# A sparse attention and maxout kernel: v in four overlapping chunks, six copies from GpSimd, and loads in order of use

## The chip, the cores and the metric

The kernel runs on one core of a Trainium2 chip. The metric is the time of one execution on the device in microseconds. A run's profile covers one execution; its span is one to two microseconds shorter than the time. TensorE does the matmuls and transposes, VectorE and ScalarE work on tiles, GpSimd ("POOL" in the profile) is a general engine, and SyncE ("SP") issues most DMA transfers. Each engine has its instructions in a fixed order, which a scheduler chooses when the program is built.

## The reference

Four batches of 8 heads, 768 positions and head size 64. Each query sees the keys within 15 positions of it, and 24 block summaries (the maximum of the keys and the mean of the values of each 32 positions). The heads' outputs are joined to rows of 512, which go through a maxout layer.

```python
k_sum = k.reshape(B, H, nb, 32, D).max(axis=3)
v_sum = v.reshape(B, H, nb, 32, D).mean(axis=3)
scores_l = where(abs(i - j) < 16, scale * q @ k.T, -1e9)
scores_s = scale * q @ k_sum.T + log(32)
a = softmax(concatenate([scores_l, scores_s]))
x = a @ concatenate([v, v_sum])           # joined over heads: [3072, 512]
out = maximum(x @ w1, x @ w2) @ w_out     # d_ff = 1024
```

## The kernel before

For each batch, `k` and `q` are loaded, cast and transposed pair by pair of heads. A tile of 64 queries needs 96 keys around it (two interleaved halves, `j`, of 48 rows of position pairs) and the 24 summaries: 120 rows, which `kext` (keys) and `vext` (values) hold for each of the 12 query tiles. `sc` are the scores, `prob` their exponentials times a 0/1 mask, `av` the product with `vext`, `x` the normalised result and `xt` its transpose, eight of them for a batch. The maxout uses `max(a, b) = a + relu(b - a)`: `wd = w2 - w1` gives `h` and `g = relu(h)`; `w1o = w1 @ w_out` is made once on the chip from `w1b` (w1 in bf16), `w1t` (its transpose) and `wo` (w_out in bf16). The maxout of one batch alternates with the attention of the next.

The values reach `vext` in this way: VectorE casts v into `vb`, with rows of position pairs in three chunks of 128. A window of 48 rows can straddle two chunks, so 16 copies within SBUF are needed for a batch, all issued by SyncE:

```python
def prep_v(b):
    vbt, vx = vb[b % 2], vext[b % 2]
    for hp in range(NP):
        nc.vector.tensor_copy(out=vbt[..., 2 * hp:2 * hp + 2, 0:D]..., in_=by_slot(loads["vf", b, hp]))
    for j in range(2):
        r = j * 48
        nc.sync.dma_start(out=vx[r:r + 48, 0], in_=vbt[0:48, 0, j])
        nc.sync.dma_start(out=vx[r:r + 48, 1:NT:4], in_=vbt[24:72, :, j])
        # ... six more copies
    ps = psum.tile([128, H, D], F32, tag="tr", bufs=2, name="vs_ps")
    # ... six matmuls with amean: block means; VectorE copies them to vx[96:NK, 0]
    nc.sync.dma_start(out=vx[96:NK, 1:NT]..., in_=vx[96:NK, 0:1]...to_broadcast(...))   # "the broadcast"
```

`kext` gets its 24 block maxima by a small GpSimd copy for each pair of heads ("the block-maximum copy"). The eight PSUM banks are `tr` 2, `sc` 2, `av` 1, `h` 2, `o` 1. The order in the program is: load batch 0, `prep_v(0)`, load the weights, attention of batch 0, cast the weights, make `w1o`, and then for each batch: load the next batch, `prep_v` of it, maxout with the next attention as its filling.

The softmax here doesn't subtract the row's maximum and nothing guards it: scores larger than these inputs give would overflow.

## Time and profile before

| | before |
|---|---|
| time, median of 3 runs | 225.22 us (224.93 to 225.33) |
| span of the profile | 224.2 us |
| TensorE busy | 174.6 us (78%) |
| first `x` started / last `xt` of batch 0 written | 37.8 / 60.2 us |
| outputs' last tile written to SBUF | 221.4 us |

In the page's second part each digit is the busy share, in tenths, of one of 40 slices of the span (5.6 us each here); PEclk is the granted TensorE clock in tenths. These are three rows of it, of the kernel before:

```profile
PE   0003832665788999896989999999999999999973
...
PEclk9999999997699999999999999999999999999999
DMA  6998438999997335999634599634431101202112
```

TensorE is full from about 80 us on. What can be won lies before that: TensorE does nothing for three slices and little up to 62 us. The DMA row shows a hole in slices 5 and 6.

The table of stretches of the same kernel: the stretch in us, its length, then the busy time and the number of instructions of PE, PEld, DVE, ACT and POOL; then the TensorE clock, the mean busy share of the DMA engines and GB/s:

```profile
0.00:20.00 20.00, 0.00 (x0) 0.10 (x1) 7.94 (x12) 1.28 (x1) 15.35 (x45) 1.00 1.01 270
20.00:40.00 20.00, 10.76 (x81) 7.56 (x81) 11.22 (x23) 8.12 (x11) 1.16 (x2) 1.00 0.55 162
40.00:62.00 22.00, 14.84 (x171) 10.95 (x172) 20.44 (x48) 11.06 (x16) 0.86 (x2) 0.84 1.04 328
62.00:80.00 18.00, 16.43 (x117) 8.88 (x116) 12.30 (x25) 6.09 (x12) 1.05 (x2) 1.00 0.68 179
80.00:115.00 35.00, 32.08 (x301) 19.19 (x304) 21.11 (x56) 17.94 (x32) 0.86 (x2) 1.00 0.78 209
```

From 20 to 40 us the DMA engines were busy for 0.55 of the time. From 40 to 62 us VectorE is busy 20.4 of 22 us and looks like the limit there. After 62 us the DMA engines have time to spare (0.68, 0.78). The timeline of SyncE (start, duration, instruction) says why there is a hole:

```profile
20.36 0.63 SPq L188 DMA_DIRECT2D vext_115<-vb_113  x1
...
31.47 0.60 SPq L195 DMA_DIRECT2D vext_115<-vb_113  x1
32.18 0.82 SPq L202 DMA_DIRECT2D vext_115<-vext_115  x1
33.05 0.53 SPq L154 DMA_DIRECT2D w2f<-in_moe_w_dram  x1
```

The sixteen copies take SyncE from 20.36 to 32.1 us. The broadcast of the means and the rest of the weights stand behind them. In the waits of TensorE (total, times, longest) the first full group of `av` waits for that broadcast, and the first `x` follows it on VectorE's timeline:

```profile
PE av L277 <- DMA vext_115<-vext_115: 4.1, 1, 4.1
```

```profile
37.79 0.56 DVE L284 TENSOR_TENSOR x<-av,inv 128x384 bf16<-128x384 f32 x1
```

### The profile page before, as it was taken

Reading aid. Unit: us, or ns where it says so; the run is one execution under the profiler, and the core shown is the slowest. Engines: PE = TensorE matmul, PEld = TensorE weight load, DVE = VectorE, ACT = ScalarE, POOL = GpSimd, SP = SyncE. Lnnn points to the kernel's source line nnn. Section 1 sums busy time; section 2 is a strip of 40 time slices with the busy share of each in tenths; the row PEclk is TensorE's granted clock in tenths of the full one; section 3 lists DMA queues with packets and bytes.
Section 4 is the critical chain, followed back from the end, with each engine's and each line's share of the span. In section 5 each row is a group of like instructions: output and inputs, shape, how many; then the busy total and the mean of one; then the engine's idle time right before and its main releaser. Section 6 shows DMA issues by size and latency. Waiting matters only on the chain.

```text
span 224.2 us, 3831 instructions
## 1 busy us (share of the span) xinstructions
PE 174.6 (78%) x1475; PEld 103.8 (46%) x1496; DVE 118.0 (53%) x268; ACT 102.7 (46%) x173; POOL 23.9 (11%) x61
## 2 busy tenths in 40 slices
PE   0003832665788999896989999999999999999973
PEld 0001622543553655664555466655546664544531
DVE  5432852899972950896857069844727853000000
ACT  2000651575120573585179248824935972442521
POOL 8990110000000010000011001000000000000000
PEclk9999999997699999999999999999999999999999
DMA  6998438999997335999634599634431101202112
GB/s 187 289 290 273 106 100 251 375 365 283 288 281 183 90 90 135 288 292 282 184 117 102 158 259 306 163 116 152 103 87 50 51 0 47 96 0 95 47 47 94
DMA packets 49858, 37.68 MB, mean 168 GB/s; under 512 B 2192, under 2 KB 44720, under 8 KB 49840
## 3 DMA queue, kind: packets, MB, share of 16 engines
q1 hardware_dynamic: 49840, 37.45, 58.5%
q8 instruction: 11, 0.18, 0.3%
q14 instruction: 7, 0.06, 0.1%
HBM read 25.17 MB, written 6.29 MB: 140 GB/s over the span
## 4 chain that ended last, share of the span: by engine, by line
PE 49%; DMA 15%; DVE 13%; ACT 11%; SPq 7%; issue 3%; POOL 1%; ACTq 0%; POOLq 0%
PE o_ps L343 16%; DMA vf<-in_v_dram 13%; PE h_ps L330 11%; PE o_ps L339 8%; PE av L277 4%; PE sc L253 2%; ACT g L332 2%; PE x_ps L294 2%; DMA vext_115<-vext_115 2%; DVE wd L161 2%; SPq L127 2%; ACT qbd_107 L242 2%; PE vs_ps L199 2%; ACT qbd_108 L242 2%; PE w1o_ps L174 2%
## 5 line engine op out<-in xcount | busy, mean ns | idle before, releaser
L330 PE MATMUL h_ps<-xt,wd 128*128 128x384 bf16 x256 | 54.2, 331 | 2.5 <-DVE xt L296 1.1
L343 PE MATMUL o_ps<-wo,g 128*128 128x512 bf16 x186 | 46.5, 379 | 0.3
L332 ACT ACTIVATE g<-h_ps 128x384 bf16<-128x384 f32 x64 | 30.1, 491 | 15.7 <-PE h_ps L330 15.2
L347 ACT COPY osb<-o_ps 128x512 f32<-128x512 f32 x24 | 14.1, 586 | 49.2 <-PE o_ps L343 49.1
L330 PEld LDWEIGHTS <-wd 128*128 128x128 bf16 x256 | 23.7, 98 | 16.8 <-issue 3.0
L343 PEld LDWEIGHTS <-g 128*128 128x128 bf16 x192 | 17.9, 98 | 18.2
L339 PE MATMUL o_ps<-w1o,xt 128*128 128x512 bf16 x83 | 24.1, 378 | 2.1 <-ACT osb L347 1.4
L199 PE MATMUL vs_ps<-vb_113,amean 128*128 128x512 bf16 x12 | 4.2, 502 | 20.4 <-DVE vb_113 L182 20.4
L282 DVE RECIPROCAL inv<-av 128x6 f32<-128x6 f32 x32 | 6.1, 190 | 25.0 <-PE av L277 24.9
L284 DVE TENSOR_TENSOR x<-av,inv 128x384 bf16<-128x384 f32 x32 | 17.6, 550 | 0.3
L234 DVE TENSOR_REDUCE ks<-k_ps 128x24 bf16<-128x768 bf16 x16 | 15.1, 945 | 0.0
L162 ACT CAST wo<-wof 128x1024 bf16<-128x1024 f32 x4 | 4.2, 1043 | 23.8 <-DMA wof<-in_moe_w_out_dram 23.8
L339 PEld LDWEIGHTS <-xt 128*128 128x128 bf16 x96 | 9.1, 97 | 10.4 <-issue 4.0
L199 PEld LDWEIGHTS <-amean 128*128 128x128 bf16 x24 | 2.5, 107 | 24.3 <-issue 13.8
L296 DVE COPY xt<-x_ps 128x384 bf16<-128x384 bf16 x32 | 11.3, 352 | 2.8 <-PE x_ps L294 2.2
L294 PE MATMUL x_ps<-identity,x 128*128 128x128 bf16 x96 | 11.2, 230 | 1.4 <-ACT qbd_108 L242 0.6
L242 ACT COPY qbd_107<-q_ps 64x768 bf16<-64x768 bf16 x10 | 7.9, 792 | 9.3 <-PE q_ps L219 9.2
L255 ACT ACTIVATE prob_109<-sc,bias 120x512 bf16<-120x512 f32 x12 | 8.3, 689 | 7.8 <-PE av L277 6.7
L242 ACT COPY qbd_106<-q_ps 64x768 bf16<-64x768 bf16 x12 | 9.5, 793 | 4.0 <-PE q_ps L219 3.9
L213 DVE CAST qb<-qf 128x768 bf16<-128x768 f32 x16 | 10.3, 647 | 1.1 <-DMA qf<-in_q_dram 1.1
L182 DVE CAST vb_113<-vf 128x768 bf16<-128x768 f32 x8 | 5.1, 638 | 10.4 <-DMA vf<-in_v_dram 10.3
L219 PE MATMUL k_ps<-identity,kb 128*128 128x128 bf16 x96 | 9.8, 236 | 1.0 <-DVE ks L234 0.9
(94 smaller groups left out, 251.0 us busy)
## 6 DMA issues: line engine op xcount, KB each, us to landing
kf<-in_k_dram SPq DMA_DIRECT2D x16, 384.0 KB
qf<-in_q_dram SPq DMA_DIRECT2D x16, 384.0 KB
vf<-in_v_dram SPq DMA_DIRECT2D x16, 384.0 KB
out_dram<-osb SPq DMA_DIRECT2D x24, 256.0 KB
w1f<-in_moe_w_dram SPq DMA_DIRECT2D x4, 512.0 KB
wof<-in_moe_w_out_dram SPq DMA_DIRECT2D x4, 512.0 KB
w2f<-in_moe_w_dram SPq DMA_DIRECT2D x4, 512.0 KB
vext_115<-vb_113 SPq DMA_DIRECT2D x8, 148.5 KB
```

The lines of the kernel that those rows point to most:

```text
L199: nc.tensor.matmul(out=ps[:], lhsT=amean[:, c, :], rhs=vbt[:, c, j, :, 0:D], start=(c == 0 and j == 0), stop=(c == 2 and j == 1))
L213: nc.vector.tensor_copy(out=qb[:], in_=by_slot(loads["qf", b, hp]))
L234: nc.vector.tensor_reduce(out=ks[:], in_=kps.rearrange("p j (n g) -> p n j g", g=16), axis=AX.XY, op=ALU.max)
L242: nc.scalar.copy(out=qx[r, :, a * 64:a * 64 + 64].rearrange("p t (g j) -> p t g j", j=2), in_=qps[r].rearrange("p j (t g) -> p t g j", g=32))
L284: nc.vector.tensor_tensor(out=x[:], in0=av[:, :, :, 0:D], in1=inv[:].to_broadcast([128, 3, 2, D]), op=ALU.mult)
L294: nc.tensor.transpose(out=ps[:, u, :], in_=xs[half][:, u].rearrange("p a d -> p (a d)"), identity=identity[:])
L296: nc.vector.tensor_copy(out=xts[b, half][:, hp, :], in_=ps[:].rearrange("p u n -> p (u n)"))
L330: nc.tensor.matmul(out=h[:], lhsT=wd[:, c, f * 128:f * 128 + 128], rhs=xt[:, c, :], start=(c == 0), stop=(c == KC - 1))
L332: nc.scalar.activation(out=g[:, f, :], in_=h[:], func=ACT.Relu)
L339: nc.tensor.matmul(out=ps[:], lhsT=xt[:, c, sl], rhs=w1o[:, c, :], start=(c == 0), stop=False)
L343: nc.tensor.matmul(out=ps[:], lhsT=g[:, f, sl], rhs=wo[:, f, :], start=False, stop=(f == FC - 1))
L347: nc.scalar.copy(out=o[:, u, :], in_=ps[:])
```

## The change

The intent: cut v into four chunks that overlap by 16 rows (112 rows each, at steps of 96), so that every window lies in one chunk, at one of three offsets in it; six copies then do what sixteen did, and one mask serves all tiles. GpSimd does the casts and issues the copies, so SyncE is free for loads; v is loaded whole, early, and the weights in halves in order of use. `vs_ps`, `w1o`, `h` and `o` share two banks (`mm`), and `av` gets two.

```diff
+    AVB, MMB, WFB = 2, 2, 8
+    NU, VP = 4, 112
+    vf = [const.tile([VP, H, 128], F32, name=f"vf{u}") for u in range(NU)]
     # ... one mask [128, 64]; edge rows of kext and vb set to zero; memsets moved to VectorE
+    def load_v(b):
+        src = v[b].rearrange("h (g j) d -> g h (j d)", j=2)
+        for u in range(NU):
+            lo, hi = max(0, 8 - 96 * u), min(VP, S // 2 + 8 - 96 * u)
+            nc.sync.dma_start(out=vf[u][lo:hi], in_=src[96 * u - 8 + lo:96 * u - 8 + hi])
     def load_batch(b):
-        for hp in range(NP):
-            for src, tag in ((k, "kf"), (q, "qf"), (v, "vf")): ...
+        load_kq(b, 0)
+        load_v(b)
+        for hp in range(1, NP):
+            load_kq(b, hp)
     def cast_weights():
         # ... in halves of d_ff
-            nc.vector.tensor_copy(out=w1b[:, c, :], in_=w1f[:])
+                nc.gpsimd.tensor_copy(out=w1b[:, c:c + 2, sl], in_=w1f[:])
                 nc.scalar.copy(out=wo[...], in_=wof[:])
     def prep_v(b):
-        # four VectorE casts, sixteen copies issued by SyncE
+        for u in range(NU):
+            nc.gpsimd.tensor_copy(out=vbt[:, u, :, :, 0:D],
+                                  in_=vf[u].rearrange("p h (j d) -> p j h d", j=2))
+        for w in range(3):
+            for j in range(2):
+                nc.gpsimd.dma_start(out=vx[j * 48:j * 48 + 48, w:NT:3],
+                                    in_=vbt[32 * w:32 * w + 48, :, j])
-        ps = psum.tile([128, H, D], F32, tag="tr", bufs=2, name="vs_ps")
+        ps = psum.tile([128, H, D], F32, tag="mm", bufs=MMB, name="vs_ps")
         # ... eight matmuls instead of six; the broadcast is issued by GpSimd
     # ... w1o_ps, h_ps, o_ps: tag "mm"; av: bufs=AVB
     def attention(b):
         prep_kq(b, 0)
         yield
+        prep_v(b)
+        yield
```

The first and last chunk load 104 rows, the two others 112.

More of the change, by code (lines that the diff above doesn't have):

```diff
@@ L54 @@
     psum = ctx.enter_context(tc.tile_pool(name="psum", bufs=1, space=bass.MemoryType.PSUM))
+    NU, VP = 4, 112
+    vf = [const.tile([VP, H, 128], F32, name=f"vf{u}") for u in range(NU)]
+    nc.vector.memset(vf[0][0:8], 0.0)
+    nc.vector.memset(vf[NU - 1][96:VP], 0.0)
     identity = const.tile([128, 128], BF16, name="identity")
     make_identity(nc, identity[:])
-    m0 = const.tile([128, 3, 64], F32, name="m0")
-    m1 = const.tile([128, 3, 64], F32, name="m1")
-    for m, j in ((m0, 0), (m1, 1)):
+    mask = const.tile([128, 64], BF16, name="mask")
@@ L65 @@
+    m1 = const.tile([128, 64], BF16, name="m1")
+    for m, j in ((mask, 0), (m1, 1)):
+        base = -16 - 95 * j
         nc.gpsimd.memset(m[:], 1.0)
-        for w, off in enumerate((0, -16, -32)):
-            base = off - 95 * j
-            sl = m[:, w, :]
-            nc.gpsimd.affine_select(out=sl, in_=sl, compare_op=ALU.is_ge, fill=0.0,
-                                    base=base + window - 1, channel_multiplier=2,
-                                    pattern=[[-1, 64]])
-            nc.gpsimd.affine_select(out=sl, in_=sl, compare_op=ALU.is_ge, fill=0.0,
-                                    base=window - 1 - base, channel_multiplier=-2,
-                                    pattern=[[1, 64]])
@@ L75 @@
-    nc.gpsimd.affine_select(out=m0[:], in_=m0[:], compare_op=ALU.is_ge, fill=0.0,
-                            base=47, channel_multiplier=-1, pattern=[[0, 3], [0, 64]])
-    nc.gpsimd.affine_select(out=m1[:], in_=m1[:], compare_op=ALU.is_ge, fill=0.0,
-                            base=-48, channel_multiplier=1, pattern=[[0, 3], [0, 64]])
-    nc.gpsimd.tensor_tensor(out=m0[:], in0=m0[:], in1=m1[:], op=ALU.add)
-    nc.gpsimd.memset(m0[96:128], 1.0)
-    mask = const.tile([128, NT, 64], BF16, name="mask")
@@ L82 @@
-    nc.gpsimd.tensor_copy(out=mask[:, 0:2, :], in_=m0[:, 0:2, :])
-    nc.gpsimd.tensor_copy(out=mask[:, NT - 2:NT, :], in_=m0[:, 1:3, :])
-    nc.gpsimd.tensor_copy(out=mask[:, 2:NT - 2, :],
-                          in_=m0[:, 1:2, :].to_broadcast([128, NT - 4, 64]))
+        nc.gpsimd.affine_select(out=m[:], in_=m[:], compare_op=ALU.is_ge, fill=0.0,
+                                base=base + window - 1, channel_multiplier=2,
+                                pattern=[[-1, 64]])
+        nc.gpsimd.affine_select(out=m[:], in_=m[:], compare_op=ALU.is_ge, fill=0.0,
+                                base=window - 1 - base, channel_multiplier=-2,
+                                pattern=[[1, 64]])
@@ L87 @@
+        nc.gpsimd.affine_select(out=m[:], in_=m[:], compare_op=ALU.is_ge, fill=0.0,
+                                base=(-48 if j else 47), channel_multiplier=(1 if j else -1),
+                                pattern=[[0, 64]])
+    nc.gpsimd.tensor_tensor(out=mask[:], in0=mask[:], in1=m1[:], op=ALU.add)
+    nc.gpsimd.memset(mask[96:128], 1.0)
     bias = const.tile([128, 1], F32, name="bias")
@@ L89 @@
     nc.gpsimd.memset(bias[96:128], logblk)
-    amean = const.tile([128, 3, 128], BF16, name="amean")
-    nc.gpsimd.memset(amean[:], 1.0 / block)
-    nc.gpsimd.affine_select(out=amean[:], in_=amean[:], compare_op=ALU.is_ge, fill=0.0,
-                            base=96 * 16, channel_multiplier=1, pattern=[[128, 3], [-16, 128]])
-    nc.gpsimd.affine_select(out=amean[:], in_=amean[:], compare_op=ALU.is_ge, fill=0.0,
-                            base=15 - 96 * 16, channel_multiplier=-1,
-                            pattern=[[-128, 3], [16, 128]])
+    amean = const.tile([VP, NU, 128], BF16, name="amean")
+    nc.vector.memset(amean[:], 0.0)
+    am = amean[:, :, 96:120]
+    nc.gpsimd.memset(am, 1.0 / block)
+    for base, mult, pat in ((-8, 1, [[96, NU], [-16, nb]]), (23, -1, [[-96, NU], [16, nb]]),
+                            (-8, 1, [[0, NU], [0, nb]]), (103, -1, [[0, NU], [0, nb]])):
+        nc.gpsimd.affine_select(out=am, in_=am, compare_op=ALU.is_ge, fill=0.0, base=base,
+                                channel_multiplier=mult, pattern=pat)
     NBUF = 3
@@ L105, with ends @@
     prob = [const.tile([128, 8 * 128], BF16, name=f"prob{i}") for i in range(NPB)]
-    vb = [const.tile([128, 3, 2, H, VW], BF16, name=f"vb{i}") for i in range(2)]
+    vb = [const.tile([VP, NU, 2, H, VW], BF16, name=f"vb{i}") for i in range(2)]
     vext = [const.tile([128, NT, H, VW], BF16, name=f"vext{i}") for i in range(2)]
+    def ends(t, a, b):
+        return (t[:, 0, a:a + 8], t[:, NT - 1, b - 8:b])
     for i in range(NBUF):
-        nc.gpsimd.memset(qbd[i][0:64, :, 64:128], 0.0)
-        nc.gpsimd.memset(qbd[i][64:128, :, 0:64], 0.0)
+        for r in (0, 64):
+            nc.vector.memset(qbd[i][r:r + 64, :, 64 - r:128 - r], 0.0)
         nc.gpsimd.memset(kext[i][:, :, NK:128], 0.0)
-    for i in range(NPB):
-        nc.vector.memset(prob[i][:], 0.0)
-    for i in range(2):
-        nc.gpsimd.memset(vb[i][:, :, :, :, D:VW], 1.0)
-        nc.gpsimd.memset(vext[i][96:NK, :, :, D:VW], 1.0)
+        for r in (0, 48):
+            for e in ends(kext[i], r, r + 48):
+                nc.gpsimd.memset(e, 0.0)
+        if i == 0:
+            for pb in prob:
+                nc.vector.memset(pb[:], 0.0)
+            for t in vb:
+                nc.gpsimd.memset(t[:, :, :, :, D:VW], 1.0)
+                nc.gpsimd.memset(t[0:8, 0, :, :, D:VW], 0.0)
+                nc.gpsimd.memset(t[96:VP, NU - 1, :, :, D:VW], 0.0)
+                nc.gpsimd.memset(t[96:104, NU - 1, :, :, D:VW], 1.0)
+            for t in vext:
+                nc.gpsimd.memset(t[96:NK, :, :, D:VW], 1.0)
     wd = const.tile([128, KC, d_ff], BF16, name="wd")
@@ L120 @@
     w1o = const.tile([128, KC, d_model], BF16, name="w1o")
-    w1b = const.tile([128, KC, d_ff], BF16, name="w1b")
-    w1t = const.tile([128, FC, d_model], BF16, name="w1t")
+    w1b = work.tile([128, KC, d_ff], BF16, tag="osb", bufs=2, name="w1b")
+    w1t = work.tile([128, FC, d_model], BF16, tag="g", bufs=2, name="w1t")
     def load_pair(src, b, hp, tag):
@@ L135, with load_kq @@
     loads = {}
+    def load_kq(b, hp):
+        for src, tag in ((k, "kf"), (q, "qf")):
+            loads[tag, b, hp] = load_pair(src, b, hp, tag)
+    def load_v(b):
[3 more added lines that the diff above has]
+            nc.sync.dma_start(out=vf[u][lo:hi], in_=src[96 * u - 8 + lo:96 * u - 8 + hi])
     def load_batch(b):
-        for hp in range(NP):
-            for src, tag in ((k, "kf"), (q, "qf"), (v, "vf")):
-                loads[tag, b, hp] = load_pair(src, b, hp, tag)
+        load_kq(b, 0)
+        load_v(b)
+        for hp in range(1, NP):
+            load_kq(b, hp)
@@ L142 @@
     wload = {}
     def load_weights():
-        w1v = moe_w1.rearrange("(kc p) n -> p kc n", p=128)
-        w2v = moe_w2.rearrange("(kc p) n -> p kc n", p=128)
-        wov = moe_w_out.rearrange("(fc p) n -> p fc n", p=128)
-        for c in range(KC):
-            w1f = stage.tile([128, d_ff], F32, tag="w1f", bufs=4, name="w1f")
-            nc.sync.dma_start(out=w1f[:], in_=w1v[:, c, :])
-            wof = stage.tile([128, 2, d_model], F32, tag="wof", bufs=2, name="wof")
-            nc.sync.dma_start(out=wof[:], in_=wov[:, 2 * c:2 * c + 2, :])
-            w2f = stage.tile([128, d_ff], F32, tag="w2f", bufs=2, name="w2f")
-            nc.sync.dma_start(out=w2f[:], in_=w2v[:, c, :])
-            wload[c] = (w1f, w2f, wof)
@@ L157, in cast_weights @@
-    def cast_weights():
-        for c in range(KC):
-            w1f, w2f, wof = wload[c]
-            nc.vector.tensor_copy(out=w1b[:, c, :], in_=w1f[:])
-            nc.vector.tensor_tensor(out=wd[:, c, :], in0=w2f[:], in1=w1f[:], op=ALU.subtract)
-            nc.scalar.copy(out=wo[:, 2 * c:2 * c + 2, :], in_=wof[:])
+        views = [w.rearrange("(c p) n -> p c n", p=128) for w in (moe_w1, moe_w2, moe_w_out)]
+        for n in range(2):
+            for c in (0, 2):
+                for w in range(3):
+                    t = stage.tile([128, 2, 512], F32, tag="wf", bufs=WFB, name="wf")
+                    if w < 2:
+                        nc.sync.dma_start(out=t[:], in_=views[w][:, c:c + 2, n * 512:n * 512 + 512])
+                    else:
+                        nc.sync.dma_start(out=t[:], in_=views[w][:, 4 * n + c:4 * n + c + 2, :])
+                    wload[w, n, c] = t
@@ new lines, in cast_weights @@
+    def cast_weights():
+        for n in range(2):
+            sl = slice(n * 512, n * 512 + 512)
+            for c in (0, 2):
+                w1f, w2f, wof = (wload[w, n, c] for w in range(3))
+                nc.vector.tensor_tensor(out=wd[:, c:c + 2, sl], in0=w2f[:], in1=w1f[:],
+                                        op=ALU.subtract)
+                nc.gpsimd.tensor_copy(out=w1b[:, c:c + 2, sl], in_=w1f[:])
+                nc.scalar.copy(out=wo[:, 4 * n + c:4 * n + c + 2, :], in_=wof[:])
@@ L171, in make_w1o @@
         for c in range(KC):
-            ps = psum.tile([128, d_model], F32, tag="o", bufs=1, name="w1o_ps")
+            ps = psum.tile([128, d_model], F32, tag="mm", bufs=MMB, name="w1o_ps")
             for f in range(FC):
@@ L180, in prep_v @@
         vbt, vx = vb[b % 2], vext[b % 2]
-        for hp in range(NP):
-            nc.vector.tensor_copy(
-                out=vbt[:, :, :, 2 * hp:2 * hp + 2, 0:D].rearrange("p c j h d -> p (c j) h d"),
-                in_=by_slot(loads["vf", b, hp]))
-        for j in range(2):
-            r = j * 48
-            nc.sync.dma_start(out=vx[r:r + 48, 0], in_=vbt[0:48, 0, j])
-            nc.sync.dma_start(out=vx[r:r + 48, 1:NT:4], in_=vbt[24:72, :, j])
-            nc.sync.dma_start(out=vx[r:r + 48, 2:NT:4], in_=vbt[56:104, :, j])
-            nc.sync.dma_start(out=vx[r:r + 40, 3:8:4], in_=vbt[88:128, 0:2, j])
-            nc.sync.dma_start(out=vx[r + 40:r + 48, 3:8:4], in_=vbt[0:8, 1:3, j])
-            nc.sync.dma_start(out=vx[r:r + 8, 4:9:4], in_=vbt[120:128, 0:2, j])
-            nc.sync.dma_start(out=vx[r + 8:r + 48, 4:9:4], in_=vbt[0:40, 1:3, j])
-            nc.sync.dma_start(out=vx[r:r + 48, NT - 1], in_=vbt[80:128, 2, j])
-        ps = psum.tile([128, H, D], F32, tag="tr", bufs=2, name="vs_ps")
-        for c in range(3):
-            for j in range(2):
-                nc.tensor.matmul(out=ps[:], lhsT=amean[:, c, :], rhs=vbt[:, c, j, :, 0:D],
-                                 start=(c == 0 and j == 0), stop=(c == 2 and j == 1))
+        for u in range(NU):
+            nc.gpsimd.tensor_copy(out=vbt[:, u, :, :, 0:D],
+                                  in_=vf[u].rearrange("p h (j d) -> p j h d", j=2))
+        for w in range(3):
+            for j in range(2):
+                nc.gpsimd.dma_start(out=vx[j * 48:j * 48 + 48, w:NT:3],
+                                    in_=vbt[32 * w:32 * w + 48, :, j])
+        ps = psum.tile([128, H, D], F32, tag="mm", bufs=MMB, name="vs_ps")
+        for u in range(NU):
+            for j in range(2):
+                nc.tensor.matmul(out=ps[:], lhsT=amean[:, u, :], rhs=vbt[:, u, j, :, 0:D],
+                                 start=(u == 0 and j == 0), stop=(u == NU - 1 and j == 1))
         nc.vector.tensor_copy(out=vx[96:NK, 0, :, 0:D], in_=ps[96:NK])
-        nc.sync.dma_start(
+        nc.gpsimd.dma_start(
             out=vx[96:NK, 1:NT].rearrange("p t h w -> p t (h w)"),
@@ L221, in prep_kq, with cols @@
                                         identity=identity[:])
-        def win(start, step, n):
-            a = kps[:, :, start:start + 48]
-            return bass.AP(a.tensor, a.offset, [a.ap[0], [step, n], a.ap[1], a.ap[2]])
-        def dst(sl):
-            return kx[:, sl, 0:96].rearrange("p t (j g) -> p t j g", j=2)
-        nc.vector.tensor_copy(out=dst(slice(1, NT - 1)), in_=win(24, 32, NT - 2))
-        nc.vector.tensor_copy(out=dst(slice(0, NT, NT - 1)), in_=win(0, 336, 2))
+        def cols(a, off, dims):
+            return bass.AP(a.tensor, a.offset + off, [a.ap[0], *dims])
+        kp = kps[:]
+        jd = [kp.ap[1][0], 2]
+        nc.vector.tensor_copy(
+            out=kx[:, 1:NT - 1, 0:96].rearrange("p t (j g) -> p t j g", j=2),
+            in_=cols(kp, 24, [[32, NT - 2], jd, [1, 48]]))
+        nc.vector.tensor_copy(
+            out=cols(kx[:], 8, [[(NT - 1) * 128 - 8, 2], [48, 2], [1, 40]]),
+            in_=cols(kp, 0, [[344, 2], jd, [1, 40]]))
         ks = work.tile([128, nb], BF16, tag="ks", bufs=2, name="ks")
@@ L259, in scores @@
         pv = pb[:NK].rearrange("p (i a n) -> p i a n", a=2, n=128)[:, :, :, 0:64]
-        mk = mask[:NK, t0:t0 + 4, :].rearrange("p i (o q) -> p i o q", o=1).to_broadcast(
+        mk = mask[:NK, :].rearrange("p (i o q) -> p i o q", i=1, o=1).to_broadcast(
             [NK, 4, 2, 64])
@@ L271, in values @@
             if u == 0:
-                avs[half] = psum.tile([128, 3, 2, D + 1], F32, tag="av", bufs=1, name="av")
+                avs[half] = psum.tile([128, 3, 2, D + 1], F32, tag="av", bufs=AVB, name="av")
             av = avs[half]
@@ L325, in maxout @@
             xt = xts[b, half]
-            g = work.tile([128, FC, 384], BF16, tag="g", bufs=2, name="g")
+            g = work.tile([128, FC, 512], BF16, tag="g", bufs=2, name="g")
             for f in range(FC):
-                h = psum.tile([128, 384], F32, tag="h", bufs=2, name="h_ps")
+                h = psum.tile([128, 384], F32, tag="mm", bufs=MMB, name="h_ps")
                 for c in range(KC):
@@ L331, in maxout @@
                                      start=(c == 0), stop=(c == KC - 1))
-                nc.scalar.activation(out=g[:, f, :], in_=h[:], func=ACT.Relu)
+                nc.scalar.activation(out=g[:, f, 0:384], in_=h[:], func=ACT.Relu)
                 yield
-            o = work.tile([128, 3, d_model], F32, tag="osb", bufs=2, name="osb")
+            o = work.tile([128, 4, d_model], F32, tag="osb", bufs=2, name="osb")
             for u in range(3):
-                ps = psum.tile([128, d_model], F32, tag="o", bufs=1, name="o_ps")
+                ps = psum.tile([128, d_model], F32, tag="mm", bufs=MMB, name="o_ps")
                 sl = slice(u * 128, u * 128 + 128)
@@ L352 @@
     load_batch(0)
-    prep_v(0)
     load_weights()
@@ L362 @@
             load_batch(b + 1)
-            prep_v(b + 1)
             side = attention(b + 1)
```

## The prediction

> **What bounds the kernel now.** By the table of stretches, from 0 to 62 us TensorE is busy 25.6 of 62 us: waiting for data, then for VectorE (busy 20.4 of 22 us from 40 to 62). From 80 to 195 us TensorE is busy 108.4 of 115 us: the limit. From 195 to 224 us it runs alone, with two 0.7 us waits for the one output bank and 3 us of eviction and store. The DMA engines are full to 20 us (share 1.01), then at 0.55 to 40 us, because SyncE issues 16 small v copies (about 0.7 us each, 20.4 to 32 us) ahead of the weights. In the timeline the first `av` group waits until 36.75 us for the last copy; batch 0's last `xt` is written at 60.2 us.
>
> **Removed.** The copies' issue time from SyncE; 16 v casts (0.57 us) and four w1 casts (0.69 us) from VectorE; the single-bank waits of `av` (about 4.5 us) and `o_ps` (1.4 us in the tail).
>
> **Added or moved.** Casts and copies go to GpSimd: 112x1024 casts at about 1.05 us each (estimate from its 128-wide cast, 0.28, and 512-wide, 0.61). Two more `vs_ps` matmuls per batch, 8 x 0.216 = 1.7 us of TensorE. v loads carry 12.5% more bytes. By the Trainium skill, "DMA: Bandwidth & Descriptors", "Why a DMA increments its semaphore by 16 and not by 1", the engine count divides the partition count, so two 104-partition loads use 13 of 16 engines; no run shows this yet. h, o, vs and w1o share two banks.
>
> **Critical path.** The freed issue time is worth little.
> 1. The new VectorE order puts three weight subtractions before the first `x` multiply. By the trace's packet durations (512 B: 31.0 ns, 264 GB/s over 16 engines; 2 KB: 89 ns, 367 GB/s; 1056 B: 68 ns, 247 GB/s), the third pair of weights lands after 18.6 us of k, q, v, 6 of v copies and 11.4 of weights: at about 38.8 us. The first `x` comes at about 40 us (before: 37.8), followed by about 19 us of VectorE work, less some overlap: last `xt` at about 58.7 us, only 1.5 us earlier.
> 2. Then `w1t` and `w1o` run without `h_ps` in their gaps (before, 25 `h_ps` matmuls were done by 69.7 us).
> 3. The new GpSimd order puts the v casts of batch 2 before the copy of block maxima for the first heads of batch 1. Those v loads land after about 75 us of full DMA work (12.4 MB at 264, 6.3 at 367, 2.7 at 247 GB/s), at about 78 us; batch 1's first `sc` starts near 80 us, and TensorE stands some 5 us. There it is about 6 us of work behind the kernel before; 0.9 us more `vs_ps` follows, the tail gives back 1.4, fewer `av` waits 1 to 2.
>
> **Time.** 228.5 us, 8 in 10 between 221 and 235. Faster by over 2%: 0.17; within: 0.45; slower: 0.38.
>
> **Signs.** Right: DMA share near 1 to 75 us; `x` near 40 us, waiting for a weight subtraction; `sc` of batch 1 waiting for GpSimd near 80 us, behind v casts that wait for their DMA. Wrong: `w1t` transposes before 55 us, or no GpSimd-caused wait of TensorE between 70 and 80 us.
>
> **What would make it wrong.** Faster DMA than the packet durations say (no stand at 75 us: about 223); GpSimd DMA issue or casts much dearer (no trace shows them): over 233; TensorE waiting for shared banks.

## The result, and the profile after

The changed kernel takes 245.3 us (fast runs 244.17, 245.31, 245.33; one slower, 248.65), the kernel before on the same chip 225.28 us. The ratio of the fast runs is 1.0872, with a 95% interval from 1.083 to 1.0915: slower by 8.7%. A ratio here is the mean time of one kernel's fast runs over the mean of the other's fast runs of the same rounds, so it is not quite the ratio of the medians. A run counts as fast if it is within 1.5% of the fastest of its kernel. The changed kernel and its relatives scatter more than the kernel before, so for them that rule leans a little to the fast side.

The same three rows of the page, of the changed kernel (slices of 6.1 us):

```profile
PE   0264100854799208789999969999999999999993
...
PEclk9999999985779855979999999999999999999999
DMA  6999999999999999999538872601220110211212
```

TensorE has two holes now, in slices 5 to 7 and 14 and 15, and the DMA row is full to slice 19. The table of stretches:

```profile
0.00:20.00 20.00, 6.06 (x28) 3.04 (x29) 11.89 (x22) 2.87 (x3) 12.84 (x57) 1.00 1.01 219
20.00:40.00 20.00, 3.23 (x28) 2.67 (x27) 6.61 (x12) 4.58 (x6) 4.85 (x7) 1.00 1.07 281
40.00:62.00 22.00, 12.49 (x155) 10.71 (x155) 17.31 (x38) 12.06 (x16) 6.32 (x7) 0.78 1.09 270
62.00:80.00 18.00, 16.37 (x117) 9.40 (x114) 12.12 (x27) 2.56 (x4) 4.54 (x7) 0.89 1.11 224
80.00:115.00 35.00, 20.81 (x172) 13.01 (x171) 11.72 (x27) 12.05 (x20) 14.34 (x18) 0.76 1.12 199
```

By 40 us TensorE has done 9.3 us of work (10.8 before). From 80 to 115 us it did 20.8 us (32.1 before), and the granted clock fell to 0.76. The sums of the DMA shares over the first 115 us are 93.6 us of full engines before and 124.8 us now (20 x 1.01 + 20 x 0.55 + ... for before). A share above 1 means that the recorded times of packets overlap on an engine, so these sums count slower packets as well as more of them. VectorE was relieved as intended (17.3 instead of 20.4 us from 40 to 62 us), but TensorE's longest waits were for others. The waits of TensorE:

```profile
PE sc L275 <- ACT prob_109 L277: 16.7, 1, 16.7
PE sc L275 <- POOL kext_101 L258: 12.1, 2, 11.8
```

These are the two large ones (a third, 11.9 us for `vb`, is mostly the start of the kernel). The first is in the prologue, and ends at 42.44 us. ScalarE's timeline shows what the exponential stood behind:

```profile
36.69 1.04 ACT L190 CAST wo<-wf 128x1024 bf16<-128x1024 f32 x1 [12.26 <-DMA wf<-in_moe_w_out_dram]
40.76 1.04 ACT L190 CAST wo<-wf 128x1024 bf16<-128x1024 f32 x1 [3.02 <-DMA wf<-in_moe_w_out_dram]
41.71 0.68 ACT L277 ACTIVATE prob_109<-sc,bias 120x512 bf16<-120x512 f32 x1
```

Two casts of w_out stand ahead of the exponential of `prob_109` in ScalarE's order. They waited 12.3 and 3.0 us for their loads, so the exponential ran at 41.7 us although its scores had long been there. But the first `x` did not wait for ScalarE alone. This is VectorE's order just before it:

```profile
43.57 1.20 DVE L187 TENSOR_TENSOR wd<-wf 128x1024 bf16<-128x1024 f32 x1
44.69 0.55 DVE L306 TENSOR_TENSOR x<-av,inv 128x384 bf16<-128x384 f32 x1
```

The third weight subtraction (`wd`) stands ahead of the first `x`. Its last weight, issued at 30.15 us, landed at 43.46 us by the trace's semaphore records, and the subtraction began 0.1 us later. (In the builds of experiments 1, 3 and 5, which have the same order there, it also began 0.1 us after that landing.) So in VectorE's order the first `x` could hardly have come before 44.7 us, whatever ScalarE did. The last `xt` of batch 0 was written at 65.4 us.

The second is seen on GpSimd. The four casts of batch 2's v (`vb_110`) stand ahead of the block-maximum copy `kext_101` of batch 1, whose input `ks` was ready at 79.1 us:

```profile
84.99 1.04 POOL L210 CAST vb_110<-vf_67 112x1024 bf16<-112x1024 f32 x1 [17.91 <-DMA vf_67<-in_v_dram]
86.42 1.04 POOL L210 CAST vb_110<-vf_68 112x1024 bf16<-112x1024 f32 x1 [0.38 <-DMA vf_68<-in_v_dram]
...
90.57 1.04 POOL L210 CAST vb_110<-vf_70 112x1024 bf16<-112x1024 f32 x1 [1.05 <-DMA vf_70<-in_v_dram]
91.55 0.43 POOL L258 COPY kext_101<-ks 128x288 bf16<-128x288 bf16 x1
```

TensorE stood until that copy was done. The four matmuls of an `h` group take 0.81 us ahead of the stand, and 1.49 us after it:

```profile
79.46 0.81 PE L354 MATMUL h_ps<-xt,wd 128*128 128x384 bf16 x4
92.04 0.61 PE L275 MATMUL sc<-qbd_104,kext_101 128*128 128x128 bf16 x4 [11.76 <-POOL kext_101 L258]
92.44 1.49 PE L354 MATMUL h_ps<-xt,wd 128*128 128x384 bf16 x4
```

That is the clock. The Trainium skill, "TensorE: Matmul & The Clock Gate", Part 1, says that the array falls to half its clock after an idle window of about 3.4 us and comes back after as much busy time. The trace agrees roughly: the records show a clock of 0.5 from 83.1 us, 2.9 us after the last matmul before the stand of 11.8 us, to 96.8 us, 4.7 us after the stand's end. They have 30.7 us at half clock in all (6.8 us before), but begin only at 49 us in this trace and at 43 us in the one before.

Why was v so late? SyncE's timeline during the loads of batch 1:

```profile
42.76 1.34 SPq L142 DMA_DIRECT2D qf<-in_q_dram  x1
44.20 2.70 SPq L160 DMA_DIRECT2D vf_67<-in_v_dram  x1
...
63.72 1.14 SPq L142 DMA_DIRECT2D qf<-in_q_dram  x1
```

A v load of 416 or 448 KB of batch 1 holds SyncE's queue for 2.3 to 2.7 us (of batch 2, for 2.5 to 4.9 us), a k or q load of 384 KB for 1.1 to 1.3 us when it does not queue behind v. The DMA records have a duration for each packet: the 512-byte packets took 31.0 ns on average before, and 39.9 ns now. Counted in stretches of 4 us, they took mostly 41 to 47 ns where the v loads of batches 0 and 1 ran, 27 to 36 ns with k and q alone, and 46 to 64 ns from 72 to 84 us, where batch 2's v was loaded, at first beside the copies.

### The profile page after: what moved, and what is told of

Its sections match the earlier page's. It is cut to its first block, busy times and chain, and to the rows that moved or that the text cites. A ratio compares the mean times of both kernels' runs of the same rounds, so it can differ in the third digit from the quotient of the medians.

```text
span 242.5 us, 3858 instructions
## 1 busy us (share of the span) xinstructions
PE 178.8 (74%) x1504; PEld 109.4 (45%) x1504; DVE 115.2 (48%) x257; ACT 104.5 (43%) x173; POOL 52.8 (22%) x112
## 3 DMA queue, kind: packets, MB, share of 16 engines
q0 software_dynamic: 1984, 5.98, 12.3%
## 4 chain that ended last, share of the span: by engine, by line
PE 48%; DMA 26%; DVE 9%; SPq 8%; issue 3%; ACT 2%; POOL 2%; POOLq 0%; ACTq 0%
PE o_ps L367 15%; PE h_ps L354 12%; PE o_ps L363 7%; DMA kf<-in_k_dram 7%; DMA wf<-in_moe_w_out_dram 7%; SPq L160 5%; DMA vext_113<-vext_113 5%; DMA vf_69<-in_v_dram 4%; PE av L299 3%; DMA vext_112<-vext_112 3%; PE sc L275 3%; SPq L177 2%; PE x_ps L316 2%; DVE ks L256 1%; PE vs_ps L219 1%
## 5 line engine op out<-in xcount | busy, mean ns | idle before, releaser
L354 PE MATMUL h_ps<-xt,wd 128*128 128x384 bf16 x256 | 52.4, 334 | 0.6 <-ACT g L356 0.6
L367 PE MATMUL o_ps<-wo,g 128*128 128x512 bf16 x192 | 47.7, 380 | 0.0
L275 PE MATMUL sc<-qbd_104,kext_101 128*128 128x128 bf16 x60 | 7.2, 255 | 28.8 <-ACT prob_109 L277 16.7
L275 PEld LDWEIGHTS <-kext_101 128*128 128x128 bf16 x60 | 4.9, 115 | 30.9 <-issue 17.4
L264 ACT COPY qbd_103<-q_ps 64x768 bf16<-64x768 bf16 x12 | 9.5, 793 | 15.9 <-PE q_ps L239 15.7
L219 PE MATMUL vs_ps<-vb_110,amean 112*128 112x512 bf16 x16 | 5.9, 494 | 11.9 <-POOL vb_110 L210 11.9
L284 DVE TENSOR_TENSOR prob_106<-prob_106,mask 120x512 bf16<-120x512 bf16 x12 | 5.5, 457 | 18.2 <-ACT prob_106 L277 18.0
L277 ACT ACTIVATE prob_106<-sc,bias 120x512 bf16<-120x512 f32 x12 | 8.2, 684 | 12.8 <-PE sc L275 11.9
L277 ACT ACTIVATE prob_109<-sc,bias 120x512 bf16<-120x512 f32 x12 | 8.3, 688 | 11.8 <-PE sc L275 11.7
L231 DVE CAST kb<-kf 128x768 bf16<-128x768 f32 x16 | 9.6, 601 | 6.2 <-DMA kf<-in_k_dram 6.2
L316 PEld LDWEIGHTS <-x 128*128 128x128 bf16 x96 | 7.5, 104 | 10.4 <-issue 4.0
L277 ACT ACTIVATE prob_107<-sc,bias 120x512 bf16<-120x512 f32 x12 | 8.2, 687 | 8.3 <-PE sc L275 8.3
```

The source lines that it names most:

```text
L275: nc.tensor.matmul(out=sc[:, i].rearrange("p a q -> p (a q)"), lhsT=kx[:, t0 + i, :], rhs=qx[:, t0 + i, :], start=True, stop=True)
L277: nc.scalar.activation(out=pb[:NK].rearrange("p (s n) -> p s n", n=128)[:, :, 0:64], in_=sc[:NK].rearrange("p i a q -> p (i a) q"), func=A ...
L316: nc.tensor.transpose(out=ps[:, u, :], in_=xs[half][:, u].rearrange("p a d -> p (a d)"), identity=identity[:])
L354: nc.tensor.matmul(out=h[:], lhsT=wd[:, c, f * 128:f * 128 + 128], rhs=xt[:, c, :], start=(c == 0), stop=(c == KC - 1))
L367: nc.tensor.matmul(out=ps[:], lhsT=g[:, f, sl], rhs=wo[:, f, :], start=False, stop=(f == FC - 1))
```

## The experiments

Twelve kernels ran, each beside the kernel before on the same chip (225.3 to 225.6 us there). "Placed behind" means an instruction of the build that fixes the order of two instructions on an engine; it changes no data and no waits on data.

### 1. The v casts placed behind the block-maximum copies

```diff
+        with (tc.issue_after(last_ks[b - 1, 3].ins) if b else ExitStack()):
             for u in range(NU):
                 nc.gpsimd.tensor_copy(out=vbt[:, u, :, :, 0:D], ...)
```

> The kernel after, with the GpSimd casts of a batch's v queued behind the block-maximum copy of the last head pair of the batch before (order in GpSimd's queue only; nothing else edited). Theory Q (the loss between 66 and 104 us is GpSimd's in-order queue: batch 2's v casts, whose data lands at 84 to 90 us, stand ahead of the copy that batch 1's first scores need): TensorE's 11.8 us wait for that copy goes, the first scores of batch 1 start at 78 to 82 us instead of 92, and the time falls by 9 to 14 us, to 231 to 236. Rival B (the DMA engines are simply too full, every path waits for its own data): batch 1's scores or av matmuls wait for other data just as long, and the time stays above 241.

233.8 us, ratio 1.0357 (1.03 to 1.0413): about 11.6 us less than the changed kernel (0.0515 of 225.3). The waits of TensorE, with the wait for `kext` gone from the top and the prologue's wait still there:

```profile
PE sc L278 <- ACT prob L280: 18.6, 2, 17.0
...
PE av L302 <- DMA vext<-vext: 7.0, 2, 4.8
```

The first scores of batch 1 started at 80.0 us instead of 92.0. So GpSimd's order was worth more than half of the loss. Nothing was removed from the work, and the other engines' orders are nearly the same in the trace (4 of VectorE's 257 instructions, 2 of ScalarE's 172 are elsewhere).

### 2. The weight casts placed behind steps of batch 0 as well

```diff
+                with tc.issue_after(last_x[0, i].ins):          # wd, VectorE
+                with tc.issue_after(last_ks[0, min(i + 2, 3)].ins):   # w1b, GpSimd
+                with tc.issue_after(last_exp[0, min(i + 1, 3)].ins):  # wo, ScalarE
```

> x1, and also the weight casts queued behind given steps of batch 0's attention on VectorE, ScalarE and GpSimd, so that no step of batch 0's attention stands behind a cast that waits for a weight. Theory W (the 5.2 us by which the last xt of batch 0 came later, 65.7 against 60.5 us, is in-order waiting behind weight casts: 16.7 us wait of the scores for the prob_109 exponential, which stood behind two wo casts): the last xt of batch 0 comes before 59 us and the time is 5 to 9 us below x1. Rival D (the prologue is bound by landing data, k and q of the later pairs and the v copies): the last xt stays above 63 us and the time is within 2 us of x1.

230.4 us, ratio 1.0188 (1.0135 to 1.024): about 3.8 us less than the first experiment, under the 5 to 9 that were expected. The first half worked: the fourth `xt` of batch 0 came at 44.2 us, 4.0 us ahead of the kernel before. (The casts of all three engines were moved at once, so this does not say which of them had to be.) Then VectorE's timeline:

```profile
61.31 1.73 DVE L191 TENSOR_TENSOR wd<-wf 128x1024 bf16<-128x1024 f32 x1 [6.80 <-DMA wf<-in_moe_w_dram]
62.96 0.34 DVE L328 COPY xt<-x_ps 128x384 bf16<-128x384 bf16 x1
```

The fourth weight subtraction stands ahead of the last `xt` and waits 6.8 us for a weight. A weight's buffer came free later, because its cast came later, so its load fell behind the loads of batch 1. The order of the casts moved the wait; it did not remove it. The last `xt` was at 63.3 us (60.2 before).

### 3. v loads of 128 whole partitions

```diff
-            lo, hi = max(0, 8 - 96 * u), min(VP, S // 2 + 8 - 96 * u)
-            nc.sync.dma_start(out=vf[u][lo:hi], in_=src[96 * u - 8 + lo:96 * u - 8 + hi])
+            lo = min(96 * u, S // 2 - 128)
+            nc.sync.dma_start(out=vf[u][:], in_=src[lo:lo + 128])
```

> The kernel after with every v load made 128 partitions wide (128 rows of the same source pattern, 8 pieces of 512 bytes, 196608 bytes apart; 18% more bytes; the rows of the first and last chunk are shifted, so the result is wrong on purpose). In the kernel after, stretches with v loads had 512-byte packets of 41 to 47 ns, stretches with only k and q 31 to 33 ns, and one v load held the queue 2.3 to 2.6 us. Theory P (the partition counts 104 and 112 cause it): packets fall to 31 to 35 ns in those stretches, a 512 KB v load holds the queue 1.7 to 1.9 us, batch 2's last v load lands 4 us or more earlier, time 238 to 243. Rival S (the source stride causes it): packets stay at 40 ns or more, v lands later still, time 245 to 250.

236.5 us, ratio 1.0437 (1.0365 to 1.0509), the result wrong (error 0.45): about 9.8 us less than the changed kernel, while it loads 19% more of v. The 512-byte packets took 30 to 35 ns in the stretches with v loads too, where no copies ran beside them (37 to 50 ns where copies did; 33.8 ns on average). GpSimd's order was left as it was: TensorE's wait for `kext` was 5.9 us instead of 11.8. Slow packets were thus a cause of v being late.

### 4. The shared banks alone

The kernel before, with `av` in two banks and `h`, `o`, `vs` and `w1o` in two shared ones.

> The kernel before with one part of the change alone: two banks for av, and h, o, vs and w1o sharing two banks. Expected if the banks cost nothing by themselves: the two 0.7 us waits of the last o_ps go, av waits of 4.5 us shrink, 222 to 225 us. Rival (sharing stops TensorE behind ScalarE and VectorE): 227 us or more.

227.7 us, ratio 1.009 (1.0049 to 1.013): a net cost of 2 us, where my prediction had counted a gain. The trace splits it. The second bank for `av` won 2.6 us by the last `xt` of batch 0 (57.5 us). Then `h`, which shares with `w1o`, no longer ran in its gaps: the fourth `g` came at 77.6 us instead of 64.6, and the eighth 3.3 us behind. The lag was 3.5 us at the 32nd `xt`; the tail, without its 1.4 us of waits for the output bank, gave some back. The scheduler's order differs in this build too, so the split is of banks with the order that comes with them.

### 5 and 6. Which partition counts are slow

Only the two middle loads at 128 partitions (correct; the cast uses 112 of them), or only the two end loads of 104 cut in 96 and 8 (96 is a multiple of 16 and 104 is not, and the prediction's point about engines turns on that).

```diff
+    VF = [VP, 128, 128, VP]                     # experiment 5
-            lo, hi = max(0, 8 - 96 * u), min(VP, S // 2 + 8 - 96 * u)
+            lo, hi = max(0, 8 - 96 * u), min(VF[u], S // 2 + 8 - 96 * u)
```

```diff
+            for a, e in (((lo, hi),) if u in (1, 2) else ((lo, lo + 96), (lo + 96, hi))):   # experiment 6
```

> The changed kernel, correct, with only the two middle v loads of each batch made 128 partitions instead of 112 (14% more bytes; the chunk still uses 112 of them); the two end loads of 104 partitions stay. Theory A (any load whose partitions are not 8 for each of the 16 DMA engines has slow packets): the two middle loads hold SyncE's queue about 1.75 us each, as in the run with all loads at 128, instead of 2.4; the end loads stay at 2.3 to 2.6; 512-byte packets lie between 34 and 40 ns in the stretches with v loads; time between 238 and 243. Rival B (only the 13-engine loads are slow, and hold up their neighbours): middle loads change to no less than 2.2 us, packets stay at 41 to 47 ns, time 244 to 247.

> The changed kernel, correct, with only the two end loads of 104 partitions each issued as 96 and 8 partitions[...]; the middle loads stay at 112. Theory A (partitions of an engine not 8): little gained, packets stay above 38 ns, time 243 to 248. Rival B (13 engines are the fault): packets fall to about 34 ns in the stretches with v loads, time 237 to 241.

| run | partitions of the v loads | 512-byte packets, mean | v loads of batch 1 hold SyncE's queue, for | time, fast runs |
|---|---|---|---|---|
| changed kernel | 104, 112, 112, 104 | 39.9 ns | 10.2 us, 1.77 MB | 244.2 to 245.3 |
| 5 | 104, 128, 128, 104 | 37.1 ns | 10.4 us, 1.90 MB | 239.2, 241.3 |
| 6 | 96+8, 112, 112, 96+8 | 39.8 ns | 11.8 us, 1.77 MB | 238.8 |
| 3 | four of 128 | 33.8 ns | 9.2 us, 2.10 MB | 234.1 to 237.2 |

(MB are partitions x 8 heads x 512 bytes.) Experiment 5: 242.9 us median, ratio of the fast runs 1.0657 (1.0576 to 1.0739). Experiment 6: 242.8 us median, but three of its four runs count as slow and no ratio was computed; adding two transfers also made the scheduler order GpSimd and VectorE otherwise, so its time tells nothing of packets. (The profiles of experiments 5 and 6 are of executions that count as slow, 244.5 and 243.1 us.) The packets' mean durations are less exposed to that, but not free of it. Cutting the 104-partition loads left them where they were, so thirteen engines for 104 partitions, which the prediction had listed as a cost, do not explain the slow packets, unless the 96s are slow for a reason of their own. Mending the two middle loads gave about half of what mending all four gave. Loads of 104 and 112, and on this showing 96, are slow alike; the queue's time in experiment 5 did not fall, which speaks against a clean halving. Why they are slow stays open. The Trainium skill, "SBUF — State Buffer", Door 1: The DMA port swizzle, says that DMA bandwidth depends on how many of the 16 SBUF ports the partitions of a load reach. By the table of ports there 96 partitions already reach all 16, so the number of ports reached does not explain these packets; no run here shows ports.

### 7. Order, banks and loads together

Experiments 1, 5 and 6 together, with the banks of the kernel before.

> The v casts placed behind the block-maximum copies of the batch before, the middle loads at 128 and the end loads split, and the PSUM banks of the kernel before (av 1, h 2, o 1). If the causes add up: 233.8 of the run with the order alone, less about 2 for the banks, less 1 to 4 for the loads: 228 to 231, still above the kernel before, for the prologue (exponential behind the w_out casts) is left in. If banks and loads only hide in other waits: 232 to 235.

236.2 us median (fast runs 233.3 and 234.3), ratio 1.0373 (1.0309 to 1.0436). It was expected at 228 to 231, and is not better than experiment 1 alone. The gains do not add. Two reasons can be seen. The packets were hardly faster (37.5 ns on average, 38.0 in experiment 1). And the 9.8 us of experiment 3 and the 11.6 us of experiment 1 are probably in large part the same microseconds, since both shorten TensorE's wait for `kext`; no run separates them. That the banks' 2 us do not show either stays open; the scatter of this kernel (233.3 to 238.2) is as large.

### 8. All orders

Experiment 7 with the weight casts of experiment 2, the fourth subtraction behind the last `xt`.

> As the last run, and the weight casts also placed behind the steps of batch 0 (the fourth weight subtraction behind the last xt, which it held up by 3 us in the run with both orders). If the prologue is the rest: last xt of batch 0 at 57 to 60 us and 222 to 226 us, even with or below the kernel before. If the weights that now load behind the loads of batch 1 only make h wait: 227 to 231.

234.0 us median (fast runs 230.8 and 232.6), ratio 1.0277 (1.0203 to 1.0351). The profile is of an execution that counts as slow (236.5 us). The last `xt` of batch 0 was at 57.1 us, as expected, 3.0 us ahead of the kernel before. But the fourth `g` was written at 77.9 us (64.6 before). The time is a little above the second alternative, but its reason is not what the trace shows: the last weight landed at 55.0 us, before the last `xt`. Instead `w1t` and `w1o` ran from 56.5 to 76.7 us (59.6 to 75.2 before), mostly ahead of the fourth `h`; TensorE waited 3.0 us there for copies of `w1t`, one of which stood behind a cast of batch 1's k that waited 2.9 us for its load. What would mend that was not tried.

### 9. The correct version with 128 partitions

As experiment 7, but all v loads of 128 partitions with a correct result: rows of the neighbouring head are read at the ends and multiplied by zero in the cast.

```diff
+                if u in (0, NU - 1):
+                    nc.gpsimd.tensor_scalar(out=vbt[:, u, :, :, 0:D], in0=vsrc,
+                                            scalar1=rm[:VP, u // 3:u // 3 + 1], scalar2=None, op0=ALU.mult)
```

> v casts behind the block-maximum copies, PSUM banks as before, and all v loads of 128 partitions with a correct result (the chunks at the ends read rows of the next or last head, which the cast multiplies by 0; only the very first and last load stay short). If packets and loads of the run with 128 partitions on purpose wrong are matched: 512-byte packets at 31 to 35 ns, v loads hold the queue about 1.75 us, time 227 to 230 (3 to 6 us under the run with split loads). If the gain there came from the order alone: 231 to 234.

236.5 us, ratio 1.0478 (1.0423 to 1.0534), no better than experiment 7. The packets were right (34.8 ns). The groups of GpSimd show what I had not costed (count, then busy time and the mean in ns):

```profile
L223 POOL TENSOR_SCALAR vb<-vf,rm 112x1024 bf16<-112x1024 f32 x8 | 24.0, 2999 | 0.5 <-DVE qbd L121 0.5
...
L227 POOL CAST vb<-vf 112x1024 bf16<-112x1024 f32 x8 | 8.2, 1053 | 0.0
```

A multiplication by one number for each partition takes GpSimd 3.0 us where the plain cast of the same tile takes 1.05. Two of them for each batch put back 3.9 us in front of the copies. That this is what used up the gain is likely, but not shown by itself. The Trainium skill, "GPSIMD Engine Reference", section 4.1, calls one-input work roughly line-rate; for the form with a scalar for each partition this run shows otherwise.

### 10. No v loads after batch 0

Experiment 7 with `load_v` for batch 0 only. Its output is wrong, which doesn't matter for the time.

> Wrong on purpose: the run with order, banks and split loads (fast runs about 233), but batches 1 to 3 use the v of batch 0, so their v loads are gone and nothing else. If full DMA engines to 115 us are what is left: the wait of av for the broadcast (4 us at 91 us) goes and so does most of the prologue's delay in loading weights only where v loads of batch 1 stood ahead of them; time 226 to 229. If what is left is order and arithmetic alone: 231 to 234.

227.6 us, ratio 1.0078 (1.0027 to 1.013): about 6.6 us less than experiment 7 (0.0295 of 225.3). Two stretches of the table, first experiment 7, then this one:

```profile
62.00:80.00 18.00, 17.59 (x121) 10.21 (x121) 11.83 (x25) 5.50 (x11) 4.56 (x8) 0.89 1.15 212
80.00:115.00 35.00, 30.11 (x291) 18.49 (x289) 21.14 (x49) 17.78 (x31) 9.79 (x13) 0.95 0.85 202
```

```profile
62.00:80.00 18.00, 17.26 (x125) 10.54 (x125) 11.30 (x24) 4.38 (x8) 3.17 (x6) 0.84 0.86 182
80.00:115.00 35.00, 33.33 (x320) 20.36 (x323) 21.18 (x50) 20.04 (x36) 9.87 (x13) 1.00 0.51 135
```

The DMA share fell from 1.15 to 0.86 and from 0.85 to 0.51, and TensorE did 3.2 us more from 80 to 115 us. The kernel before loads v as well, but had room for it there (0.68 and 0.78). So this is what the v loads of batches 1 to 3 cost in this arrangement. What the old loads cost in the kernel before was not tried, so it is not the price of the new loads against the old ones.

### 11. The kernel before, with half of batch 0's copies issued by GpSimd

Here one idea of the change is put alone into the kernel before: do not let one engine issue all the copies.

```diff
     for j in range(2):
         r = j * 48
-        nc.sync.dma_start(out=vx[r:r + 48, 0], in_=vbt[0:48, 0, j])
+        eng = nc.gpsimd if b == 0 and j == 1 else nc.sync
+        eng.dma_start(out=vx[r:r + 48, 0], in_=vbt[0:48, 0, j])
         # ... the seven others likewise
```

> The kernel before with one idea of the change alone: of the 16 copies of batch 0, the 8 of the odd rows are issued by GpSimd, the others and all later batches stay on SyncE. If issue time in the prologue is worth something: SyncE is at the broadcast by about 27 us instead of 32, first av at 31 to 33 us instead of 36.75, last xt at 55 to 58 instead of 60.5, time 220 to 223. If VectorE (20.4 of 22 us) or DMA takes it back: first av earlier, last xt within 1 us, time 224 to 226.

221.6 us (221.56 to 222.77), ratio 0.9838 (0.979 to 0.9886): correct, and faster than both kernels, 1.6% under the kernel before. SyncE was at the broadcast at 27.72 us instead of 32.18:

```profile
19.90 0.65 SPq L189 DMA_DIRECT2D vext<-vb  x1
...
27.72 0.82 SPq L203 DMA_DIRECT2D vext<-vext  x1
```

GpSimd issued its eight in the same time, and was done before the first block-maximum copy:

```profile
24.50 0.54 POOL L196 DMA_DIRECT2D vext<-vb  x1
25.21 0.60 POOL L237 COPY kext<-ks 128x288 bf16<-128x288 bf16 x1 [0.17 <-DVE ks L235]
```

The first `x` follows at 33.53 us instead of 37.79:

```profile
33.53 0.56 DVE L285 TENSOR_TENSOR x<-av,inv 128x384 bf16<-128x384 f32 x1
```

The last `xt` of batch 0 came at 55.0 us (60.2), and a lead of 4.4 us is left at the last output tile. (The scheduler ordered VectorE and TensorE otherwise in this build too; the lead at the first `x` follows the earlier broadcast, 4.5 us, and what comes after it is of both.) The DMA share from 20 to 40 us was 0.83 instead of 0.55. The Trainium skill, "DMA: Bandwidth & Descriptors", Issuing engines are not separate DMA queues, says that issuing from several engines only saves the time of issuing, which is usually small beside the transfer. The trace agrees with the first part; here the time was not small, because sixteen issues of about 0.7 us stood in front of the broadcast.

### 12. The same, and the w1 casts on GpSimd

```diff
-            nc.vector.tensor_copy(out=w1b[:, c, :], in_=w1f[:])
+            with tc.issue_after(last_ks[0, min(c + 2, 3)].ins):
+                nc.gpsimd.tensor_copy(out=w1b[:, c, :], in_=w1f[:])
```

> As the last run, and the four w1 casts moved from VectorE to GpSimd, each placed behind a block-maximum copy so that none of those waits for a weight. If VectorE bounds 40 to 62 us: 1 to 3 us less than the last run, 218 to 222. If not: the same as the last run.

223.5 us, ratio 0.9918 (0.987 to 0.9965): 1.9 us worse than experiment 11, against an expected gain. GpSimd ran three of the casts in a row:

```profile
47.94 4.19 POOL L162 CAST w1b<-w1f 128x1024 bf16<-128x1024 f32 x3
```

In just that time, VectorE's operations with two inputs in SBUF became slow: the mask multiplication, else 0.41 us, took 2.43 us for two, and the subtraction, else 1.2 us, 1.71:

```profile
44.50 0.42 DVE L265 TENSOR_TENSOR prob<-prob,mask 120x512 bf16<-120x512 bf16 x1
...
48.35 1.71 DVE L163 TENSOR_TENSOR wd<-w2f,w1f 128x1024 bf16<-128x1024 f32 x1
49.98 2.43 DVE L265 TENSOR_TENSOR prob<-prob,mask 120x512 bf16<-120x512 bf16 x2
...
52.60 0.41 DVE L265 TENSOR_TENSOR prob<-prob,mask 120x512 bf16<-120x512 bf16 x1
```

The Trainium skill, "SBUF — State Buffer", Who interferes with whom, says that a VectorE instruction with two SBUF inputs contends with a GpSimd instruction that reads SBUF, and that such contention is an exclusive lock. The trace agrees; so does the changed kernel's, where the same multiplication took 1.04 and 1.23 us at 42.4 and 46.3 us, beside GpSimd's w1 casts. Work moved from VectorE to GpSimd was not all gone from VectorE here.

## Why the prediction was right or wrong

The prediction gave 228.5 us with a range of 221 to 235; it was 245.3. It had the mechanism of the main loss, and two of its terms were far off. In the profiled executions (spans 242.5 and 224.2 us):

| term | predicted | measured |
|---|---|---|
| last `xt` of batch 0, against before | 1.5 us earlier | 5.3 us later (65.4 against 60.2) |
| TensorE's stand before `sc` of batch 1 | 5 us | 11.8 us |
| the rest up to the sixth output tile (the "about 6 us behind" less the two above) | 2.5 us | 3.1 us (20.2 us behind there) |
| from there to the last output tile | about 2 us gained back | 2.2 us gained back |
| sum | +3.3 us as recorded (the terms give 4) | +17.9 us (before rounding) |

- **Step 1 failed: "the third pair of weights lands" at about 38.8 us, "The first `x` comes at about 40 us", the last `xt` "at about 58.7 us".** The weights landed at 43.5 us, the first `x` came at 44.7 and the last `xt` at 65.4. The path on VectorE was right: the third subtraction stands before the first `x` and began as its weight landed. The term that failed is the time to that landing, 4.7 us too short. The step took 31.0 ns for each 512-byte packet and 89 ns for each of 2 KB; up to 43.5 us they took 38.6 and 102 ns. For the 9,600 packets of 512 bytes alone that is 4.5 us over 16 engines (an estimate from the trace; packets overlap). From the first `x` to the last `xt` it took 20.7 us where the step had 18.7.
- **Step 1 also left out ScalarE's order**, where two w_out casts stand before an exponential (15.3 us of waiting for loads). That held TensorE until 42.4 us, but it was over before the subtraction, so it lies under the late weights and does not by itself explain the first `x`. Experiments 2 and 8 place the casts of all three engines later: the fourth `xt` then came 4.0 us ahead of the kernel before instead of 5.5 us behind (experiment 2), the last 3.0 us ahead (experiment 8). Which engine's casts count for how much was not tried.
- **Step 3 was right in kind and mis-sized in two numbers: "at about 78 us" and "TensorE stands some 5 us".** GpSimd's order did hold the block-maximum copy behind batch 2's casts (experiment 1, 11.6 us). But v landed from 85 to 90.6 us, and the stand was 11.8 us. The term that was mis-sized is the DMA's again: I took 31.0 ns for every 512-byte packet from a kernel whose loads all have 128 partitions, and the packets of the v loads took 41 to 47 ns (of batch 2, more). An estimate from the trace: the 10,368 v packets of three batches, 12 ns more each, over 16 engines, are 7.8 us. The copies add to it: their 4224-byte packets took 330 ns, 205 GB/s over 16 engines, where I had used 247. Experiment 3 confirms the packets' part.
- **The thirteen engines for 104 partitions**: the prediction drew this on the skill's page. Experiment 6 split those loads and the packets stayed at 39.8 ns, so the count alone does not explain the slowness. No record tells which engine moved a packet, so the count itself is not shown.
- **GpSimd's costs were right**: casts of 1.04 us (estimated 1.05), and a DMA issue of about 0.6 us, no dearer than SyncE's.
- **The banks were put on the wrong side.** "Fewer `av` waits" and the tail were counted as gains; experiment 4 shows those gains (2.6 us early, some in the tail) and a larger loss in between, a net cost of 2 us on the kernel before.
- **"The freed issue time is worth little" was wrong as a general statement.** In the changed kernel no gain of it was left. In the kernel before, halving SyncE's copies for batch 0 was worth 3.7 us (experiment 11), the whole lead being there at the first `x`.
- **Half clock was not in the prediction.** 30.7 us at half clock are on record, the longest of them after the stand. How much of the loss that is was not tried by itself. TensorE's busy times (174.6 and 178.8 us) do not tell it: the trace of the kernel before lacks 21 of its 1496 matmul records.

Step 2 was right: `w1t` and `w1o` ran from 64.7 to 75.9 us, and the first `h` group began only at 75.8 us. Of the signs that the prediction named, the full DMA to 75 us, the `sc` of batch 1 behind v casts that wait for their DMA (at 92 us, not 80), and `w1t` after 55 us were all seen. The sign for step 1 was seen late: `x` behind a weight subtraction, at 44.7 us instead of 40.

What stays open: why loads of 96, 104 and 112 partitions have slower packets; and why experiments 7 and 8, with the known causes mended, still lie 2.8 to 3.7% above the kernel before. Experiment 10 shows that the v loads of the later batches cost 6.6 us in that arrangement, but not how much more than the old ones; and experiment 8 moved the last `xt` of batch 0 forward without a shorter time to the fourth `g`.

## What to carry to other kernels

When work is moved to another engine, read the new order on *every* engine and ask of each instruction that waits for a load what stands behind it: here casts and subtractions for later use held up a small copy, an exponential and the first `x`, and placing them later won back 15.4 of the 19.6 us (experiments 1 and 2). Cost a transfer with the packets of its own shape, not of another's, and do not add up gains that shorten the same wait. If one part of a change has a clear purpose, try it alone: splitting sixteen issues over two engines, one line of the idea, gave 1.6%, and the whole change lost 8.7%.

## What the Trainium skill lacked or had wrong

- "DMA: Bandwidth & Descriptors" and "SBUF — State Buffer": loads from HBM of 104 and 112 partitions have 512-byte packets of mostly 41 to 47 ns, against 27 to 36 ns for 128 partitions in the same kernel. The first page ties a partition count to a number of engines; splitting 104 into 96 and 8 changed nothing (39.8 against 39.9 ns on average). The second advises 128 but gives no measured figure between 64 and 128 partitions.
- "DMA: Bandwidth & Descriptors": copies within SBUF issued by GpSimd with 4224-byte packets moved 205 GB/s over 16 engines (330 ns each) beside the loads, slower than 1056-byte packets issued by SyncE in a kernel with less traffic (68 ns, 247 GB/s). And the issue time that several issuing engines save, called usually small relative to the transfer, was 4.5 us here.
- "GPSIMD Engine Reference": a 112x1024 cast from f32 took 1.05 us, the same tile times one scalar for each partition 3.0 us; section 4.1 calls one-input work roughly line-rate and does not set the two apart.
- "SBUF — State Buffer", Who interferes with whom, was right: two mask multiplications took 2.43 us, else 0.41 us each, beside GpSimd's casts.
- "TensorE: Matmul & The Clock Gate" was right on the fall to half clock (0.81 to 1.49 us for an `h` group after a stand of 11.8 us; 30.7 of 242.5 us at half clock by the records).
